# Convolution and SiLU MLP: the up projection by a seven-product block scheme in 64-row tiles

## The chip, the cores and the metric

The kernel runs on one core of one Trainium2 chip. What is measured is the device time of one execution in microseconds (us). Beside the timed runs there is one profiled execution, in which the hardware records every instruction of every engine; all rows shown come from it. Engines are named as in the profile: PE is TensorE (its weight loads, PEld, are a row of their own), DVE is VectorE, ACT is ScalarE, POOL is GpSimd, and SP is the engine whose queue issues most transfers here.

## The reference

Two steps. The first is a causal convolution over the sequence, with seven taps for each of 8 heads (24 channels a head), the taps being a softmax of the weights. The second is an MLP: up from 192 to 2048 channels, SiLU, and down to 192. Everything is fp32.

```python
x: (8, 4096, 192)   weight: (8, 7)   w_in: (192, 2048)   w_out: (2048, 192)
w = softmax(weight, axis=-1)                  # 7 taps per head
conv[b, s, h, :] = sum_k w[h, k] * x[b, s + k - 6, h, :]   # zeros before the start
h = conv.reshape(32768, 192) @ w_in           # "up"
g = h / (1 + exp(-h))                         # SiLU
out = g @ w_out                               # "down"
```

The two weight matrices arrive in 8-byte floats and are rounded to fp32 on the chip, by integer arithmetic on VectorE (`round_w`).

## The kernel before

The 32768 tokens are worked off in 64 blocks of 512. A block goes through these stages:

- `load` (L78): x comes in by eight transfers on SP's queue, in pieces of 32 tokens by 32 channels. `turn_in` (L187) transposes 32x32 squares on VectorE, so that channels lie on the 128 rows (partitions) and tokens along the row. 192 channels make one piece of 128 rows and one of 64; the 64 are held twice, in the lower and the upper half of the rows. Six boundary tokens of the block before are put in front (L184, on POOL).
- `conv` (L198, L200): seven taps for each of the two pieces, one multiplication and six multiply-adds of 128x512 on VectorE.
- Up: the 2048 channels are 16 chunks of 128. For a chunk, `up_a` (L207) contracts the 128-row piece and `up_b` (L215) adds the remaining 64 rows into the same PSUM bank. `up_b` runs for two chunks at a time, one on the lower 64 rows of the array and one on the upper 64: a product on 64 rows uses half of the array, and two on different halves can run side by side.
- `act` (L225): ScalarE reads the bank and writes SiLU of it to SBUF as `g`, one instruction of 128x512 a chunk.
- Down: `down` (L234) contracts each chunk's `g` with w_out, four pieces of 128 tokens, each 192 columns, into two accumulator banks that are open for the whole block.
- `store`: VectorE copies the accumulators (L246), one transfer writes the block.

A block handles its chunks in two groups of eight: four L207, eight L215 (four that finish the first four chunks, four that begin the next four), four L207, then the down products of the eight. PSUM has eight banks: six rotate for h, two are the accumulators.

The program text is unrolled. A planner, ahead of the run, gives every engine a fixed order of instructions and puts the waits between engines; the order of the text counts as priority, but where it reckons an instruction ready early it puts it earlier. So the transposes of a coming block stand directly behind the taps of the one before, and in the first block the rounding steps, transposes and taps are interleaved. At run time each engine takes its queue in that order. A tile can be written again only when a buffer of its pool (`bufs`) is free: all readers of the earlier content are done.

In the first block the weights are loaded and rounded: eight passes (`round_w`, L129 to L149) of twelve VectorE instructions of 768 columns each. One pass covers the up and down weights of two chunks.

Of the kernel before, what the change touches and what calls it, by code (L numbers as in the profile page):

```python
# [16 lines left out]
def kernel(  # L17
# [20 lines left out]

    nc = tc.nc
# [7 lines left out]
    R = D - P  # L47
    grp = D // H
    pad = K - 1
    SUBS = 4  # L50
    TB = P * SUBS
    NB = NT // TB
    NCH = DFF // P
    NQ = NCH // 2
    GA = 4
    assert NCH % (2 * GA) == 0 and GA % 2 == 0
    assert R == 64 and D == H * grp and S % TB == 0 and DFF == 2 * P * NQ and NQ >= 3

    SQ = 32
# [4 lines left out]
    wpool = ctx.enter_context(tc.tile_pool(name="wp", bufs=3))  # L64
    xpool = ctx.enter_context(tc.tile_pool(name="xp", bufs=3))
    gpool = ctx.enter_context(tc.tile_pool(name="gp", bufs=3 * GA))
    opool = ctx.enter_context(tc.tile_pool(name="op", bufs=2))
    ps_h = ctx.enter_context(tc.tile_pool(name="ps_h", bufs=6, space=PSUM))
    ps_o = ctx.enter_context(tc.tile_pool(name="ps_o", bufs=1, space=PSUM))

    nats, xts, cvs, hs, gs, accs = ({} for _ in range(6))

    def load(b):
        nat = nats[b] = xpool.tile([P, 2, TB // SQ, SQ], F32, tag="nat", name="nat")
        for half in range(2):
            for i in range(P // SQ):
                c = SQ * i if half == 0 else P + SQ * i % R
                nc.sync.dma_start(  # L78
                    out=nat[SQ * i : SQ * i + SQ, half, :, :], in_=x_v[b][:, :, c : c + SQ]
                )  # L80

    load(0)


    wraw = const.tile([P, 2, K], F32, name="wraw")
    for half, p0, c0, c1 in ((0, 0, 0, P), (1, 0, P, D), (1, R, P, D)):
        c = c0
        while c < c1:
            h = c // grp
            e = min((h + 1) * grp, c1)  # L90
            p = p0 + c - c0
            nc.scalar.dma_start(
                out=wraw[p : p + e - c, half, :],
                in_=weight[h : h + 1, :].to_broadcast([e - c, K]),
            )
            c = e
# [3 lines left out]
    WA, WB, WO = 2 * P, 3 * P, 3 * P + 2 * D  # L100
    in32 = moe_w_in.bitcast(I32)
    out32 = moe_w_out.bitcast(I32).rearrange("(q e p) d -> q p e d", e=2, p=P)
    raws = {}

    def load_w(q):
        raw = raws[q] = wpool.tile([P, 2 * WO], I32, tag="raw", name="raw")
        nc.gpsimd.dma_start(out=raw[:, 0 : 2 * WA], in_=in32[0:P, 4 * P * q : 4 * P * q + 4 * P])  # L107
        for e in range(2):
            c = 2 * P * (2 * q + e)
            nc.gpsimd.dma_start(  # L110
                out=raw[R * e : R * e + R, 2 * WA : 2 * WB], in_=in32[P:D, c : c + 2 * P]
            )
        nc.gpsimd.dma_start(  # L113
            out=raw[:, 2 * WB : 2 * WO].rearrange("p (e d) -> p e d", e=2), in_=out32[q]
        )

    ws = [const.tile([P, WO], F32, name=f"w{q}") for q in range(NQ)]

    def round_w(q):
        words = raws.pop(q).rearrange("p (n t) -> p n t", t=2)  # L120
        lo, hi = words[:, :, 0], words[:, :, 1]
        sc, ex, mh, ml, st = (
            wpool.tile([P, WO], I32, tag=f"w_{n}", name=f"w_{n}", bufs=1)
            for n in ("sc", "ex", "mh", "ml", "st")
        )
        m = wpool.tile([P, WO], F32, tag="w_m", name="w_m", bufs=1)

# [24 lines left out]

    def w_in_a(q, e):
        return ws[q][:, ts(e, P)]

    def w_in_b(q, e):
        return ws[q][R * e : R * e + R, WA:WB]

# [150 lines left out]
```

## Time and profile before

| | |
|---|---|
| median of 3 runs | 2759.59 us (2758.9 to 2760.28) |
| the profiled execution's own time | 2759.42 us |
| its span, first to last instruction | 2757.4 us |
| TensorE (PE) busy | 2708.0 us, 98% |
| weight loads (PEld) busy | 1908.8 us, 69% |
| VectorE (DVE) busy | 765.9 us, 28% |
| ScalarE (ACT) busy | 573.2 us, 21% |
| GpSimd (POOL) busy | 36.0 us, 1% |
| granted TensorE clock, mean | 0.998 of full |

How to read the rows. In a row of the page's group list stand the line of the kernel, the engine, the operation, what it writes and reads (by the program's names), the shapes, the count; then busy time in us and the mean of one in ns; then the idle time of the engine before these instructions, and what ended most of it. In a timeline row stand the start in us, the length in us, engine, line, operation and count; neighbours of one kind are merged, and a bracket names the idle time before and what released it. A windows row gives a stretch of time, its length, the busy time (and count) of PE, PEld, DVE, ACT and POOL, the granted clock, the share of the DMA engines that was busy, and GB/s. A row of transfers gives the count, the size of one and the median time from issue to landing. Matmuls are pipelined: the length of one is more than its distance to the next, so distances between starts are the better price.

### The profile page before, as it was taken

How to read it: one execution, taken by the hardware profiler on the slowest of the kernel's cores; microseconds unless marked ns; L12 is line 12 of the kernel's file. 1: busy time of each engine (PE TensorE's matmuls, PEld its weight loads, DVE VectorE, ACT ScalarE, POOL GpSimd, SP SyncE). 2: the span in 40 equal slices, each digit the busy share in tenths (PEclk: the TensorE clock that was granted, in tenths of full speed). 3: DMA queues.
4: the chain of work that ended last, by engine and by line, in shares of the span. 5: the costliest groups of instructions: out<-in, count | busy, mean ns of one | idle time of the engine just before them, and what ended most of it. 6: DMA issues, size and time to landing. Idle time of an engine off the chain costs nothing.

```text
span 2757.4 us, 29182 instructions
## 1 busy us (share of the span) xinstructions
PE 2708.0 (98%) x12288; PEld 1908.8 (69%) x12288; DVE 765.9 (28%) x1254; ACT 573.2 (21%) x1027; POOL 36.0 (1%) x100
## 2 busy tenths in 40 slices
PE   3999999999999999999999999999999999999999
PEld 2666776776677667767776776677667767776776
DVE  8613223223133132231231321322313313223120
ACT  1122112211221221122112211221221122112211
POOL 3000000000000000000000000000000000000000
PEclk9999999999999999999999999999999999999999
DMA  5211011011110110110101101101101011000000
GB/s 130 37 27 27 14 27 27 14 27 22 19 27 14 27 28 14 28 27 14 27 19 22 27 14 27 27 14 27 26 15 28 15 26 27 14 19 12 6 12 12
DMA packets 306711, 66.92 MB, mean 24 GB/s; under 512 B 272276, under 2 KB 305172, under 8 KB 306580
## 3 DMA queue, kind: packets, MB, share of 16 engines
q1 hardware_dynamic: 304128, 58.76, 10.8%
q0 software_dynamic: 2048, 6.29, 0.8%
q8 instruction: 96, 1.57, 0.2%
q14 instruction: 35, 0.29, 0.0%
q10 hardware_dynamic: 404, 0.01, 0.0%
HBM read 39.85 MB, written 25.17 MB: 24 GB/s over the span
## 4 chain that ended last, share of the span: by engine, by line
PE 97%; DVE 3%; DMA 0%; issue 0%; DVEq 0%
PE acc L234 48%; PE h L207 32%; PE h L215 17%; DVE cv L200 1%; DMA nat<-in_x_dram 0%; DVE w_ex L129 0%; DVE w L149 0%; DVE w_m L146 0%; DVE w_m L143 0%; DVE w_sc L136 0%; DVE w_st L142 0%; DVE w_st L141 0%; DVE w_sc L129 0%; DVE w_mh L129 0%; DVE w_ml L140 0%
## 5 line engine op out<-in xcount | busy, mean ns | idle before, releaser
L234 PEld LDWEIGHTS acc<-w,g 128*128 128x128 f32 x8192 | 1338.1, 190 | 67.2 <-issue 62.7
L234 PE MATMUL acc<-w,g 128*128 128x192 f32 x8192 | 1353.7, 326 | 1.4 <-ACT g L225 1.4
L225 ACT ACTIVATE g<-h 128x512 f32<-128x512 f32 x1024 | 570.4, 600 | 2158.0 <-PE h L215 1837.3
L207 PE MATMUL h<-cv,w 128*128 128x512 f32 x2048 | 938.3, 601 | 40.3 <-DVE w L149 40.3
L207 PEld LDWEIGHTS h<-cv,w 128*128 128x128 f32 x2048 | 375.6, 190 | 506.0 <-issue 465.1
L198 DVE TENSOR_SCALAR cv<-xt,taps 128x512 f32<-128x512 f32 x128 | 56.6, 483 | 1889.2 <-PE h L207 1889.2
L200 DVE SCALAR_TENSOR_TENSOR cv<-xt,taps,cv 128x512 f32<-128x512 f32 x768 | 514.8, 745 | 0.0
L215 PE MATMUL h<-cv,w 64*128 64x512 f32 x2048 | 476.0, 603 | 3.4 <-DVE w L149 3.4
L215 PEld LDWEIGHTS h<-cv,w 64*128 64x128 f32 x2048 | 198.6, 186 | 270.6 <-issue 247.0
L246 DVE COPY osb<-acc 128x384 f32<-128x384 f32 x128 | 63.7, 532 | 85.0 <-PE acc L234 84.6
L187 DVE STREAM_TRANSPOSE xt<-nat 128x512 f32<-128x512 f32 x128 | 83.8, 691 | 5.0
L184 POOL COPY xt<-xt 128x12 f32<-128x12 f32 x56 | 12.5, 223 | 2171.6 <-DVE cv L200 2146.3
L110 POOL DMA_DIRECT2D raw<-in_moe_w_in_dram x16 | 9.5, 603 | 0.0
L129 DVE TENSOR_SCALAR w_ex<-w_ex 128x768 int32<-128x768 int32 x16 | 8.8, 549 | 0.0
L136 DVE TENSOR_TENSOR w_sc<-w_sc,w_ex 128x768 int32<-128x768 int32 x8 | 7.6, 946 | 0.0
L149 DVE SCALAR_TENSOR_TENSOR w<-w_m,w_sc 128x768 f32<-128x768 f32 x8 | 7.5, 943 | 0.0
L146 DVE SCALAR_TENSOR_TENSOR w_m<-w_mh,w_m 128x768 f32<-128x768 int32 x8 | 7.5, 940 | 0.0
L143 DVE SCALAR_TENSOR_TENSOR w_m<-w_ml,w_st 128x768 f32<-128x768 int32 x8 | 7.5, 937 | 0.0
L107 POOL DMA_DIRECT2D raw<-in_moe_w_in_dram x8 | 6.4, 803 | 38.7 <-DVE w_st L141 37.9
L129 DVE TENSOR_SCALAR w_ex<-raw 128x768 int32<-128x768 int32 x8 | 4.4, 551 | 7.8 <-DMA raw<-in_moe_w_out_dram 7.8
L113 POOL DMA_DIRECT2D raw<-in_moe_w_out_dram x8 | 6.3, 791 | 0.3 <-DMA raw<-in_moe_w_out_dram 0.3
L182 POOL MEMSET xt<- 128x12 f32 x8 | 1.2, 145 | 293.9 <-DVE cv L200 293.9
(18 smaller groups left out, 26.2 us busy)
## 6 DMA issues: line engine op xcount, KB each, us to landing
nat<-in_x_dram SPq DMA_DIRECT2D x512, 64.0 KB, 2.4
out_dram<-osb SPq DMA_DIRECT2D x64, 384.0 KB, 2.8
raw<-in_moe_w_out_dram POOLq DMA_DIRECT2D x8, 384.0 KB, 5.1
raw<-in_moe_w_in_dram POOLq DMA_DIRECT2D x8, 256.0 KB, 3.8
raw<-in_moe_w_in_dram POOLq DMA_DIRECT2D x16, 64.0 KB, 3.2
wraw<-in_weight_dram ACTq DMA_DIRECT2D x9, 0.7 KB
wraw<-in_weight_dram ACTq DMA_DIRECT2D x2, 0.4 KB
wraw<-in_weight_dram ACTq DMA_DIRECT2D x1, 0.2 KB
```

The costliest lines, as they stand in the source:

```text
L110: nc.gpsimd.dma_start(out=raw[R * e : R * e + R, 2 * WA : 2 * WB], in_=in32[P:D, c : c + 2 * P])
L129: nc.vector.tensor_scalar(out, in_, scalar1=s1, scalar2=s2, op0=op0, op1=op1)
L136: nc.vector.tensor_tensor(sc, sc, ex, op=ALU.bitwise_or)
L184: nc.gpsimd.tensor_copy(xt[:, :, 0:pad], xts[b - 1][:, :, TB : TB + pad])
L187: nc.vector.transpose(xt[:, half, pad : pad + TB], nat[:, half, :, :].rearrange("p k c -> p (k c)"))
L198: nc.vector.tensor_scalar(dst, src[:, 0:TB], scalar1=tap, scalar2=None, op0=ALU.mult)
L200: nc.vector.scalar_tensor_tensor(out=dst, in0=src[:, k : k + TB], scalar=tap, in1=dst, op0=ALU.mult, op1=ALU.add)
L207: nc.tensor.matmul(hs[b, c], w_in_a(c // 2, c % 2), cvs[b][:, 0, :], start=first, stop=not first)
L215: nc.tensor.matmul(hs[b, 2 * q + e], w_in_b(q, e), cvs[b][R * e : R * e + R, 1, :], start=first, stop=not first,)
L225: nc.scalar.activation(gs[b, c], hs.pop((b, c)), AF.Silu)
L234: nc.tensor.matmul(accs[b][s // 2][:, s % 2, :], g[:, ts(s, P)], w_out(c), start=c == 0 and s % 2 == 0, stop=c == NCH - 1, skip_group_chec ...
L246: nc.vector.tensor_copy(osb[:, 2 * i : 2 * i + 2, :], acc)
```

## The change

Blocks become 1024 tokens (two halves of 512, called n = 0 and 1). The 192 channels become three thirds of 64 rows. x is held as 128 rows, of which the lower 64 are one third of the channels for the first token half and the upper 64 the same third for the second half; so the convolution works on three pieces of 128x512 for 1024 tokens. Its results are then copied by transfers on SP (`dups`), so that each third of each token half lies on the lower and on the upper 64 rows.

The 16 chunks of 128 output channels become 8 pairs: chunk m with chunk 8 + m. For a pair, the two token halves and the first two thirds of the contraction, the up products form a 2x2 by 2x2 block product; from the second block on (`up_pair`) it is computed with seven products instead of eight (P1 to P7). It needs combinations of the weights (`combine`, once, on POOL), of the convolved input (`win`, four subtractions on VectorE a block), and of the results: U2, U3 and the final sums, five additions of 128x512 on VectorE for each pair, one operand in PSUM, and one copy on ScalarE. The last third is done plainly, four products (E11, E12, E21, E22). Every product is on 64 rows; the order written out in `up_pair` puts one on each row half in every slot. The first block does the plain twelve products (`up_plain`).

All PSUM tiles come from one pool of eight banks. Down is the same products in another order of chunks, eight pieces of 128 tokens in four accumulator banks. Rounding takes eight VectorE and two ScalarE instructions a pass; w_in and w_out are rounded separately. x, convolution and output tiles have one buffer each.

```diff
-    TB = P * SUBS
-    NB = NT // TB
+    TB = 512
+    TT = 2 * TB
+    SUBS = TT // P
+    NB = NT // TT
...
+    xpool = ctx.enter_context(tc.tile_pool(name="xp", bufs=1))
+    gpool = ctx.enter_context(tc.tile_pool(name="gp", bufs=NCH))
+    upool = ctx.enter_context(tc.tile_pool(name="up", bufs=6))
+    psum = ctx.enter_context(tc.tile_pool(name="ps", bufs=8, space=PSUM))
...
+    def rounded(dst, key):
...
+        nc.vector.tensor_single_scalar(ex, hi, 0x7FF * one, op=ALU.bitwise_and)
+        nc.vector.tensor_single_scalar(st, lo, 0xFF, op=ALU.bitwise_and)
+        nc.vector.tensor_scalar(
+            ex, ex, scalar1=float(896 * one), scalar2=float(1151 * one), op0=ALU.max, op1=ALU.min
+        )
+        nc.scalar.sign(st, st)
+        nc.scalar.activation(ex, ex, AF.Copy, bias=-float(896 * 8 * one), scale=8.0)
...
+    def combine(j):
+        def comb(out, u, v, op):
+            nc.gpsimd.tensor_tensor(out, u, v, op=op)
+        s, r = ws[j], wr[j]
+        comb(s[:, 1, 0, :], s[:, 1, 0, :], s[:, 1, 1, :], ALU.add)
+        comb(s[:, 0, 0, :], s[:, 1, 0, :], s[:, 0, 0, :], ALU.subtract)
...
     def turn_in(b):
...
+        for k in range(NK):
             nc.vector.transpose(
+                xt[:, k, pad : pad + TB], nat[:, k, :, :].rearrange("p k c -> p (k c)")
             )
+        nc.sync.dma_start(out=xt[R:P, :, 0:pad], in_=xt[0:R, :, TB : TB + pad])
+        if (b + 1) * TT % S:
+            tails[b + 1] = xpool.tile([R, NK, pad], F32, tag="tail", name="tail", bufs=2)
+            nc.sync.dma_start(out=tails[b + 1], in_=xt[R:P, :, TB : TB + pad])
...
+    def conv(b, k):
...
+        for n in range(2):
+            for e in range(2):
+                nc.sync.dma_start(
+                    out=dups[b][R * e : R * e + R, n, k, :], in_=cvs[b][R * n : R * n + R, k, :]
+                )
...
+    def win(b):
+        d = dups[b]
+        t = wins[b] = xpool.tile([P, 4, TB], F32, tag="win", name="win")
+        for i, u, v in (
+            (0, d[:, 1, 0, :], d[:, 0, 0, :]),
+            (1, d[:, 1, 1, :], t[:, 0, :]),
+            (2, d[:, 1, 1, :], d[:, 1, 0, :]),
+            (3, d[:, 0, 1, :], t[:, 1, :]),
+        ):
+            nc.vector.tensor_tensor(t[:, i, :], u, v, op=ALU.subtract)
...
+    def up_pair(b, j):
+        d, t = dups[b], wins[b]
+        r, s = wr[j], ws[j]
+        prods = {
+            "P1": (0, r[:, 0, 0, :], d[:, 0, 0, :], "b", True),
+            "P2": (0, r[:, 0, 1, :], d[:, 0, 1, :], "b", False),
+            "E11": (0, r[:, 0, 2, :], d[:, 0, 2, :], "b", False),
+            "P7": (0, r[:, 1, 0, :], t[:, 2, :], "c", True),
+            "P4": (0, r[:, 1, 1, :], t[:, 3, :], "c", False),
+            "E21": (0, r[:, 1, 2, :], d[:, 0, 2, :], "c", False),
+            "P6": (1, s[:, 0, 0, :], t[:, 1, :], "a", True),
+            "P5": (1, s[:, 1, 0, :], t[:, 0, :], "d", True),
+            "E22": (1, s[:, 1, 2, :], d[:, 1, 2, :], "d", False),
+            "P3": (1, s[:, 0, 1, :], d[:, 1, 1, :], "d", False),
+            "E12": (1, s[:, 0, 2, :], d[:, 1, 2, :], "d", False),
+        }
...
+        def after(e, name):
+            top, low = 2 * j + e, NM + 2 * j + e
+            if name == "P1":
+                us[e, 2] = upool.tile([P, TB], F32, tag="u", name="u")
+                nc.scalar.copy(us[e, 2], bk[e, "b"])
+            elif name == "E11":
+                nc.scalar.activation(g_tile(b, top)[:, 0, :], bk[e, "b"], AF.Silu)
+            elif name == "U2":
+                add(us[e, 2], us[e, 2], bk[e, "a"])
+            elif name == "U3":
+                us[e, 3] = upool.tile([P, TB], F32, tag="u", name="u")
+                add(us[e, 3], us[e, 2], bk[e, "c"])
+            else:
+                c, n, u, bn = {
+                    "E22": (low, 1, 3, "d"), "E21": (low, 0, 2, "c"), "E12": (top, 1, 2, "d")
+                }[name]
+                g = g_tile(b, c)[:, n, :]
+                add(g, us[e, u], bk[e, bn])
+                nc.scalar.activation(g, g, AF.Silu)
+        for slot, then in (
+            (((0, "P1"), (0, "P6")), ((0, "P1"),)),
+            (((0, "P7"), (0, "P5")), ((0, "U2"), (0, "U3"))),
+            (((1, "P6"), (1, "P1")), ((1, "P1"),)),
+            (((1, "P5"), (0, "E22")), ((0, "E22"), (1, "U2"))),
+            (((1, "E22"), (1, "P7")), ((1, "U3"), (1, "E22"))),
+            (((0, "P2"), (1, "P2")), ()),
+            (((0, "E11"), (0, "P3")), ((0, "E11"),)),
+            (((0, "P4"), (0, "E12")), ((0, "E12"),)),
+            (((0, "E21"), (1, "E11")), ((0, "E21"), (1, "E11"))),
+            (((1, "P3"), (1, "P4")), ()),
+            (((1, "E12"), (1, "E21")), ((1, "E12"), (1, "E21"))),
+        ):
+            for e, name in slot:
+                mm(e, name)
+            for e, name in then:
+                after(e, name)
...
     for b in range(NB):
+        for j in range(NJ):
             if b == 0:
+                round_in(j)
...
+                up_plain(b, j)
+            else:
+                up_pair(b, j)
+        if b == 0:
+            for q in range(NCH // 4):
+                round_out(q)
...
+        if b + 1 < NB:
+            turn_in(b + 1)
+            if b + 2 < NB:
                 load(b + 2)
+            for k in range(NK):
+                conv(b + 1, k)
+            win(b + 1)
+        if b == 0:
+            for j in range(NJ):
+                combine(j)
+        accs = down(b)
+        store(b, accs)
```

341 lines of the change are left out of this document (183 added, 158 removed).

## The prediction

> **What bounds the kernel now.** I read the page's totals first, then the chain that ended last, then the costliest groups.
>
> ```profile
> span 2757.4 us, 29182 instructions
> PE 2708.0 (98%) x12288; PEld 1908.8 (69%) x12288; DVE 765.9 (28%) x1254; ACT 573.2 (21%) x1027; POOL 36.0 (1%) x100
> PE 97%; DVE 3%; DMA 0%; issue 0%; DVEq 0%
> L234 PE MATMUL acc<-w,g 128*128 128x192 f32 x8192 | 1353.7, 326 | 1.4 <-ACT g L225 1.4
> L225 ACT ACTIVATE g<-h 128x512 f32<-128x512 f32 x1024 | 570.4, 600 | 2158.0 <-PE h L215 1837.3
> L207 PE MATMUL h<-cv,w 128*128 128x512 f32 x2048 | 938.3, 601 | 40.3 <-DVE w L149 40.3
> L200 DVE SCALAR_TENSOR_TENSOR cv<-xt,taps,cv 128x512 f32<-128x512 f32 x768 | 514.8, 745 | 0.0
> L215 PE MATMUL h<-cv,w 64*128 64x512 f32 x2048 | 476.0, 603 | 3.4 <-DVE w L149 3.4
> L246 DVE COPY osb<-acc 128x384 f32<-128x384 f32 x128 | 63.7, 532 | 85.0 <-PE acc L234 84.6
> L187 DVE STREAM_TRANSPOSE xt<-nat 128x512 f32<-128x512 f32 x128 | 83.8, 691 | 5.0
> L136 DVE TENSOR_TENSOR w_sc<-w_sc,w_ex 128x768 int32<-128x768 int32 x8 | 7.6, 946 | 0.0
> ```
>
> TensorE is busy for 98% of the span and holds 97% of the chain; VectorE and ScalarE are idle for over 70%. Each fp32 matmul call is two instructions (1024 calls of L207 are 2048). So only TensorE time counts, as long as nothing new makes it wait. The timeline of TensorE in the middle of the run gives its rhythm (start, length up to the last result, line, count):
>
> ```profile
> 1012.38 10.56 PE L234 MATMUL acc<-w,g 128*128 128x192 f32 x64
> 1022.78 3.60 PE L207 MATMUL h<-cv,w 128*128 128x512 f32 x8
> 1026.31 3.70 PE L215 MATMUL h<-cv,w 64*128 64x512 f32 x16
> 1029.94 3.70 PE L207 MATMUL h<-cv,w 128*128 128x512 f32 x8
> 1033.48 10.56 PE L234 MATMUL acc<-w,g 128*128 128x192 f32 x64
> ```
>
> One round, 1012.38 to 1033.48, is 21.10 us: 10.40 of down and 10.70 of up (3.53 + 3.63 + 3.54). It covers 512 tokens and half of the 2048 channels, so 1024 tokens cost 84.4 us: 41.6 down, 42.8 up. The two ends of the run (last down, last copy):
>
> ```profile
> 27.74 3.40 PE L207 MATMUL h<-cv,w 128*128 128x512 f32 x4 [27.74 <-DVE w L149]
> 94.45 3.60 PE L207 MATMUL h<-cv,w 128*128 128x512 f32 x8
> 2742.44 10.56 PE L234 MATMUL acc<-w,g 128*128 128x192 f32 x64
> 2752.39 1.21 DVE L246 COPY osb<-acc 128x384 f32<-128x384 f32 x2 [40.99 <-PE acc L234]
> 0.00:50.00 50.00, 18.81 (x72) 11.23 (x72) 41.55 (x74) 6.15 (x9) 20.83 (x35) 1.00 0.67 148
> 50.00:100.00 50.00, 36.15 (x138) 21.11 (x140) 48.67 (x81) 6.56 (x12) 4.23 (x6) 0.90 0.25 53
> 1000.00:1084.60 84.60, 84.60 (x387) 59.86 (x386) 22.09 (x36) 17.82 (x32) 0.39 (x2) 1.00 0.11 22
> ```
>
> The first 512 tokens last until 94.45; the other 63 blocks take 126 rounds, 2658.6 us, and end at 2753.0; copy and store add 4.4. In the first 100 us VectorE (fourth number of a windows row, 41.55 and 48.67 of 50) rounds the weights and TensorE (the second) waits. In the steady stretch TensorE is busy for all of 84.60 us, VectorE for 22.09.
>
> **The change, part by part.** *Up.* A pair of chunks, two token halves and three thirds of the contraction would be 12 products of 64 rows. The new scheme replaces the 8 products of the first two thirds by 7 and keeps 4 of the last: 11, so 1/12 of the up work goes, not 1/8. A block has 8 chunk pairs, 88 products, issued as 44 slots of two, one on each row half. Their price has a row now, the weight loads inside an L215 run, where two 64-row tiles go side by side:
>
> ```profile
> 2693.61 0.19 PEld L215 LDWEIGHTS h<-cv,w 64*128 64x128 f32 x2 [0.24 <-issue]
> 2694.04 0.19 PEld L215 LDWEIGHTS h<-cv,w 64*128 64x128 f32 x2 [0.23 <-issue]
> 2694.47 0.19 PEld L215 LDWEIGHTS h<-cv,w 64*128 64x128 f32 x2 [0.23 <-issue]
> 2694.89 0.19 PEld L215 LDWEIGHTS h<-cv,w 64*128 64x128 f32 x2 [0.24 <-issue]
> 2694.29 2.06 ACT L225 ACTIVATE g<-h 128x512 f32<-128x512 f32 x4 [14.29 <-PE h L215]
> ```
>
> Three steps take 1.28 us, 0.427 for one instruction on each half, so a slot (two instructions on each) is 0.853. 44 slots are 37.6 us. The run of 16 lasts 3.63 against 8 x 0.427 = 3.41, so entering 64-row tiles costs about 0.2, once a block now; L207's 3.53 puts about 0.1 on the change between up and down. Up is 37.9, down stays 41.6 (the same 256 instructions), a block 79.5 instead of 84.4: 4.9 us, for 31 blocks 152 us.
>
> The skill speaks against pricing by perfect pairs. The Trainium skill (TensorE: Matmul & The Clock Gate, "Measured speedup vs the span model") gives 3.07x, not 4x, for four row tiles of 512 columns. At that efficiency, an estimate from the page, 37.6 would become 49.0, the block 90.9 and the time 2938; rival C is that case. In the trace the pair of halves steps at the 0.427 of the four rows above, so I take the row.
>
> *New VectorE work.* Each chunk pair adds five additions of 128x512, one operand in PSUM; a channel group j (two pairs, 11 slots, 9.4 us) has ten. No such instruction is in the trace. Bounds: the PSUM copy of 384 columns, 532 ns, below; the 768-column two-operand L136, 946 ns, above. I take 745 ns, the 512-column two-operand L200: 7.5 us of 9.4. At 946 ns they would fill 9.5 us, the break-even, so even the upper bound stalls little. The slots leave room: the sum from the fourth slot is needed out of its bank before the seventh, 1.7 us for two additions; the last two banks of a group are wanted three slots, 2.6 us, after their last product, and need two additions, 1.5.
>
> ScalarE gets a copy per pair and keeps four 512-column Silu: ten instructions of 600 ns, 6.0 of 9.4 us. A wait there holds the Silu queued behind it, and then a bank; cover is 3.4 us a group.
>
> *Convolution and its copies.* Per 1024 tokens, three pieces of seven taps instead of four, three transposes instead of four, four subtractions: VectorE 21 + 4 two-operand-like and 3 transposes. Steady rows of now:
>
> ```profile
> 1012.65 0.88 DVE L198 TENSOR_SCALAR cv<-xt,taps 128x512 f32<-128x512 f32 x2 [31.19 <-PE h L207]
> 1013.45 8.03 DVE L200 SCALAR_TENSOR_TENSOR cv<-xt,taps,cv 128x512 f32<-128x512 f32 x12
> 1021.58 1.30 DVE L187 STREAM_TRANSPOSE xt<-nat 128x512 f32<-128x512 f32 x2
> 1066.39 4.04 SPq L78 DMA_DIRECT2D nat<-in_x_dram  x7
> nat<-in_x_dram SPq DMA_DIRECT2D x512, 64.0 KB, 2.4
> out_dram<-osb SPq DMA_DIRECT2D x64, 384.0 KB, 2.8
> L184 POOL COPY xt<-xt 128x12 f32<-128x12 f32 x56 | 12.5, 223 | 2171.6 <-DVE cv L200 2146.3
> ```
>
> Twelve taps in 8.03 are 0.66 apiece back to back: conv 3 x (0.4 + 6 x 0.66) = 13.1, transposes 1.9, subtractions 2.6: 17.6 us, beside 41.6 of down. The next block's row copies (12 transfers of 128 KB on SP) cannot overwrite their one buffer before the last up product, so they start with down: at 0.58 us an issue (4.04 for 7) and 2.8 to land, 10 us. If the conv of the block after waits for them, 10 + 17.6 is still under 41.6: hidden, cover 14 us. SP's x loads, 12 for 1024 tokens instead of 16, stand behind them and are wanted a block later. PSUM is now one pool of eight banks: the four accumulators are free again, by copies of 0.53, by the third slot of the next block, 1.7 us in. Cost zero; without the cover it is 0.5 us a block.
>
> *First block.* It runs the plain 12 products. A rounding pass is four one-operand and four two-operand steps, with two steps on ScalarE, instead of eight and four. Rows of three consecutive steps:
>
> ```profile
> 59.88 0.55 DVE L129 TENSOR_SCALAR w_mh<-raw 128x768 int32<-128x768 int32 x1
> 60.35 0.95 DVE L136 TENSOR_TENSOR w_sc<-w_sc,w_ex 128x768 int32<-128x768 int32 x1
> 61.22 0.55 DVE L140 TENSOR_SCALAR w_ml<-raw 128x768 int32<-128x768 int32 x1
> ```
>
> 0.47 and 0.87 from start to start: 5.4 us a pass instead of 7.2, eight passes 43 instead of 58. Before the first product stand one pass, the transposes, the small copy of the six boundary tokens (2.4 by the nat row), one conv piece of 4.4 and its row copy (2.8): I take a first product at 26, as 27.74 now; the other two conv pieces hold TensorE for about 2 more, a cold clock for 2 (its four first instructions took 3.40). 48 slots are 41.0, down 41.6: 113 us. Passes of 6 us, with the ScalarE steps in them, keep ahead of groups of 10.2 us. Bounds: 105 with no wait, 140 if every pass after the first stood 4 us in TensorE's way. Now 1024 tokens end at 94.45 + 42.2 = 136.7. The twenty weight combinations on POOL, unpriced in the trace (its only copy, L184, has 12 columns), have the first down to hide in: they cost nothing up to 2 us each.
>
> **Sum.** 113 + 31 x 79.5 (2464.5) + 4.8 for the last copies and store = 2582.3 of span; the profiled execution took 2759.42 for its span of 2757.4, 2.0 more, so 2584. It stands 0.2 us under the median of 2759.59.
>
> **Rivals.**
>
> *A. The additions come late in some slots.* Chain: product, ScalarE copy, two or three additions, the next product into the same bank. For it: five ordered steps where there was one Silu, and VectorE at 80% in this stage; one filler instruction of 0.66 ahead of an addition eats a third of the 1.7 us. Against: 14.29 us of ScalarE idle now and slack at every place I priced. At 0.66 us a group, one late addition, 2.6 us a block, 82 us: 2666.
>
> *B. VectorE becomes the bound of the up stage: slower.* The order of the VectorE queue is planned ahead; if it puts the next conv between the additions, up holds 29.8 + 17.6 = 47.4 us of VectorE work against 37.9 of TensorE. The block becomes 89.0 and the time 113 + 2759 + 7 = 2879. It decides from 43.5 us of VectorE work in up, where the 5.6 us a block gained in all (175 / 31) are used up. For it: now the taps are issued as soon as a buffer is free. Against: that buffer comes free only with the row copies at the start of down. The Trainium skill (TensorEngine Tiling (Array Packing), "PSUM Bottleneck") warns of just this, that packing speeds the array but not the emptying of PSUM.
>
> *C. The halves fall apart: slower.* If a product waits alone while its partner runs, the slot costs 1.71 instead of 0.853. With a quarter of the slots so, 11 x 0.853 = 9.4 us a block, 2875; break-even at 6.6 of 44. Against: L215's runs stay paired now, though their products also wait for banks; but they have no VectorE step between them.
>
> *D. The count is right but the start is not:* the first block at 140 instead of 113, 2611. It lies inside the forecast's own range.
>
> **Numbers.** Forecast with D 0.69, A 0.17, B 0.08, C 0.06. Less than 0.2%, 5.5 us, cannot be told from no change. Faster: the forecast and A but for its worst end, 0.85; same 0.02; slower: B and C nearly whole, 0.13. The predicted time is 2584. The forecast's own range is 2566 (first block 105, block 79.2) to 2640 (first block 140, 80.4 a block); A's middle extends the 8-in-10 range to 2685, leaving most of B and C and the worst of A out.
>
> **What would show it.** Right: TensorE over 97% busy, up stretches of 176 instructions in about 38 us between down stretches of 41.6, additions of 0.7 to 0.75 us, taps and subtractions inside down, a first pair product of the second block near 113. A shows as idle TensorE in front of up products, released by VectorE; B as taps between additions and VectorE busy through up; C as up stretches with TensorE busy but far over 38 us. Wrong altogether: a block over 84.4 us.

## The result and the profile after

The changed kernel takes 2642.19 us (median of 4 runs, 2641.86 to 2644.18) against 2759.44 us of the kernel before, measured beside it (2758.9 to 2760.28). The ratio is 0.9576, 95% interval 0.956 to 0.9593: 117 us less. The forecast was 2584, 175 us less; its own range was 2566 to 2640, widened to 2685 for rival A.

The page of the changed kernel, its totals, the chain and the groups of the new additions:

```profile
span 2640.4 us, 34007 instructions
PE 2576.4 (98%) x13840; PEld 2045.2 (77%) x13840; DVE 1466.8 (56%) x2270; ACT 780.4 (30%) x1355; POOL 33.7 (1%) x77
PE 97%; DMA 1%; DVE 1%; POOL 0%; ACT 0%; issue 0%; ACTq 0%; SPq 0%; DVEq 0%; POOLq 0%
L334 DVE TENSOR_TENSOR g<-u,ps 128x512 f32<-128x512 f32 x744 | 491.4, 684 | 231.6 <-PE ps L328 227.2
L334 DVE TENSOR_TENSOR u<-u,ps 128x512 f32<-128x512 f32 x496 | 331.9, 685 | 185.3 <-ACT u L340 170.5
```

TensorE still sets the time. VectorE's busy time has nearly doubled, from 765.9 to 1466.8 us; most of what is new are the 1240 additions of L334, at 684 ns where the forecast took 745. TensorE's timeline shows where the span goes, first at the beginning, then in the middle:

```profile
43.46 6.57 PE L292 MATMUL ps<-dup,wr 64*128 64x512 f32 x16 [43.46 <-DMA dup<-cv]
53.38 10.20 PE L292 MATMUL ps<-dup,wr 64*128 64x512 f32 x32 [3.35 <-DMA dup<-cv]
76.66 34.46 PE L292 MATMUL ps<-dup,wr 64*128 64x512 f32 x144 [13.08 <-ACT g L302]
111.05 41.87 PE L384 MATMUL ps<-wo,g 128*128 128x192 f32 x256
152.85 0.69 PE L328 MATMUL ps<-dup,wr 64*128 64x512 f32 x1
...
1034.28 0.69 PE L328 MATMUL ps<-dup,wr 64*128 64x512 f32 x1
...
1049.21 0.69 PE L328 MATMUL ps<-dup,ws 64*128 64x512 f32 x1
1049.41 0.59 PE L328 MATMUL ps<-dup,wr 64*128 64x512 f32 x1
1049.75 0.59 PE L328 MATMUL ps<-dup,ws 64*128 64x512 f32 x1
...
1072.58 41.87 PE L384 MATMUL ps<-wo,g 128*128 128x192 f32 x256
1114.38 0.69 PE L328 MATMUL ps<-dup,wr 64*128 64x512 f32 x1
```

A block in the middle runs from 1034.28 to 1114.38: 80.10 us, 38.30 of up and 41.80 of down. The second block begins at 152.85 instead of 113. With 31 blocks of 80.10, what is left of the span is 4.45, nearly all of it the last copies and the store. So the 58 us that the forecast has too little are 39.85 in the first block and 31 x 0.6 = 18.6 in the others, less 0.35 at the end.

**The first block.** Three things are late. First, the first product, at 43.46 instead of 26. VectorE's and SP's rows:

```profile
14.07 0.56 DVE L132 TENSOR_SCALAR w_ex<-raw 128x768 int32<-128x768 int32 x1 [7.68 <-DMA raw<-in_moe_w_in_dram]
21.09 0.55 DVE L132 TENSOR_SCALAR w_ex<-raw 128x768 int32<-128x768 int32 x1
28.92 0.70 DVE L233 STREAM_TRANSPOSE xt<-nat 128x512 f32<-128x512 f32 x1
32.92 8.82 DVE L251 SCALAR_TENSOR_TENSOR cv<-xt,taps,cv 128x512 f32<-128x512 f32 x12
31.35 8.67 SPq L83 DMA_DIRECT2D nat<-in_x_dram  x12
41.10 15.02 SPq L256 DMA_DIRECT2D dup<-cv  x12
```

Rounding starts only at 14.07, when the weights have landed. Then a whole second pass (21.09 to 27.5) and the beginning of a third stand ahead of the third transpose, and the taps of two convolution pieces are interleaved, so that neither is done before 41. On SP's queue twelve loads of x for the second block are issued ahead of the first row copy; they end at 40.0, in time for these late pieces and in the way of earlier ones.

Second, TensorE stands for 13.08 us, released at 76.66 by a Silu. ScalarE's rows around it, and the step on VectorE that precedes:

```profile
70.32 0.56 DVE L133 TENSOR_SCALAR w_st<-raw 128x768 int32<-128x768 int32 x1 [1.31 <-DMA raw<-in_moe_w_out_dram]
73.86 0.84 ACT L138 ACTIVATE w_ex<-w_ex 128x768 int32<-128x768 int32 x1 [2.10 <-DVE w_ex L134]
74.72 1.28 ACT L302 ACT_TABLE_LOAD   x1
76.01 2.07 ACT L302 ACTIVATE g<-ps 128x512 f32<-128x512 f32 x4
```

The banks were full at 63.6 and their Silu could have begun then. But in ScalarE's queue the two steps of seven rounding passes stand ahead of the first Silu, and the seventh, of w_out, has its first VectorE step at 70.32. A queue runs in its order, so the Silu begins at 76.01.

Third, the clock. Windows of the same execution (stretch; busy time of PE, PEld, DVE, ACT, POOL; granted clock; DMA):

```profile
63.60:76.60 13.00, 0.00 (x0) 0.00 (x0) 11.69 (x17) 5.24 (x7) 3.14 (x5) 0.58 0.79 175
76.60:90.00 13.40, 13.34 (x48) 11.21 (x50) 13.40 (x22) 8.26 (x16) 0.00 (x0) 0.77 0.01 2
```

Over the wait the granted clock averages 0.58, and over the stretch behind it 0.77. From 43.46 to 111.05 are 67.59 us; less the two waits 51.16 remain for 192 instructions, which take 41.40 in the warm twelve-product run below. The 9.8 us over it are three slow starts, some 3.3 us each. Behind the two waits the granted clock shows it (0.73 from 53.38 to 63.60, and 0.77 above). For the first start it does not: the windows give 1.00 from 43.46 to 50.03, though 16 instructions take 6.57 us there, where the warm pace of 41.40 for 192 gives 3.5. That this start too is slow by the clock is argued from the like pace, not shown.

**The other blocks.** The product at 1049.21 is P3 of the first pair in its group. It writes into the bank that the addition for E22 reads:

```profile
1046.48 2.08 DVE L334 TENSOR_TENSOR u<-u,ps 128x512 f32<-128x512 f32 x3 [1.17 <-ACT u L340]
1048.48 0.68 DVE L334 TENSOR_TENSOR g<-u,ps 128x512 f32<-128x512 f32 x1
```

This addition ends at 1049.16, and P3 follows. Three additions stand ahead of it on VectorE, not two: behind U2 and U3 of the first pair the third can only be U2 of the second pair, which the planner put in front of the E22 sum. Without its 0.60 us the sum would have ended at 1048.56, before P3's turn at 1049.41 - 0.43 = 1048.98, when its partner started (an estimate from these rows; that order was not run). The other half did not wait: its next instruction starts at 1049.41, the partner only at 1049.75, and the two halves stay 0.34 us apart. It happens once a block and is most of the 0.4 us by which up is longer than 37.9.

### The profile page after: what moved, and what is told of

Its sections match the earlier page's. It is cut to its first block, busy times and chain, and to the rows that moved or that the text cites. A ratio compares the mean times of both kernels' runs of the same rounds, so it can differ in the third digit from the quotient of the medians.

```text
span 2640.4 us, 34007 instructions
## 1 busy us (share of the span) xinstructions
PE 2576.4 (98%) x13840; PEld 2045.2 (77%) x13840; DVE 1466.8 (56%) x2270; ACT 780.4 (30%) x1355; POOL 33.7 (1%) x77
## 4 chain that ended last, share of the span: by engine, by line
PE 97%; DMA 1%; DVE 1%; POOL 0%; ACT 0%; issue 0%; ACTq 0%; SPq 0%; DVEq 0%; POOLq 0%
PE ps L384 51%; PE ps L328 45%; PE ps L292 1%; DVE cv L251 1%; DMA raw<-in_moe_w_in_dram 0%; DMA nat<-in_x_dram 0%; DMA ws<-wr 0%; DMA raw<-in_moe_w_out_dram 0%; POOL ws L173 0%; DMA xt<-xt 0%; DVE w_ex L151 0%; POOL raw L115 0%; DVE w_mh L148 0%; DVE xt L233 0%; DVE w_ex L132 0%
## 5 line engine op out<-in xcount | busy, mean ns | idle before, releaser
L384 PEld LDWEIGHTS ps<-wo,g 128*128 128x128 f32 x8192 | 1330.3, 190 | 24.3 <-issue 24.3
L384 PE MATMUL ps<-wo,g 128*128 128x192 f32 x8192 | 1339.8, 326 | 0.0
L328 PE MATMUL ps<-dup,wr 64*128 64x512 f32 x1984 | 736.9, 591 | 0.0
L328 PE MATMUL ps<-dup,ws 64*128 64x512 f32 x1488 | 679.8, 591 | 0.0
L334 DVE TENSOR_TENSOR g<-u,ps 128x512 f32<-128x512 f32 x744 | 491.4, 684 | 231.6 <-PE ps L328 227.2
L354 ACT ACTIVATE g<-g 128x512 f32<-128x512 f32 x744 | 461.6, 630 | 415.1 <-DVE g L334 414.7
L328 PE MATMUL ps<-win,wr 64*128 64x512 f32 x992 | 505.0, 589 | 0.0
L328 PEld LDWEIGHTS ps<-dup,wr 64*128 64x128 f32 x1984 | 308.9, 187 | 201.0 <-issue 138.0
L334 DVE TENSOR_TENSOR u<-u,ps 128x512 f32<-128x512 f32 x496 | 331.9, 685 | 185.3 <-ACT u L340 170.5
L328 PE MATMUL ps<-win,ws 64*128 64x512 f32 x992 | 427.1, 592 | 0.0
L292 PE MATMUL ps<-dup,wr 64*128 64x512 f32 x192 | 51.2, 683 | 59.9 <-DMA dup<-cv 46.8
L292 PEld LDWEIGHTS ps<-dup,wr 64*128 64x128 f32 x192 | 39.2, 219 | 71.1 <-DVE w_mh L148 43.4
```

The costliest lines, as they stand in the source:

```text
L292: nc.tensor.matmul(hs[a, n, e], rows(wr[j], e)[:, a, k, :], rows(d, e)[:, n, k, :], start=k == 0, stop=k == NK - 1,)
L328: nc.tensor.matmul(bk[e, bn], rows(w, half), rows(v, half), start=first, stop=True, skip_group_check=True,)
L334: nc.vector.tensor_tensor(out, u, v, op=ALU.add)
L354: nc.scalar.activation(g, g, AF.Silu)
L384: nc.tensor.matmul(accs[s // 2][:, s % 2, :], g[:, ts(s, P)], wo[c // 4][:, c % 4, :], start=i == 0 and s % 2 == 0, stop=i == NCH - 1, ski ...
```

## The experiments

In the expectations, Theory 1 is this reading: the scheme runs at its price in the steady blocks but for the slip of P3, and the rest was lost in the first block to the order of queues. The rivals are named with each.

| kernel | time, us | ratio to the kernel before, 95% interval |
|---|---|---|
| changed kernel | 2642.19 | 0.9576 (0.956 to 0.9593) |
| twelve products | 2738.13 | 0.9922 (0.9907 to 0.9937) |
| twelve products, halves in turn | 3667.59 | one run |
| every addition twice | 3199.33 | 1.1594 (1.157 to 1.1617) |
| four more additions, early | 2847.45 | 1.0319 (1.0302 to 1.0337) |
| four more additions, late | 2638.93 | 0.9562 (0.9548 to 0.9577) |
| P3 a slot later | 2633.76 | 0.9542 (0.9528 to 0.9557) |
| rounding without ScalarE | 2629.11 | 0.9526 (0.9512 to 0.954) |
| start in order | 2629.32 | 0.9526 (0.951 to 0.9542) |
| these three together | 2617.00 | 0.9484 (0.9469 to 0.9498) |
| and two further queues mended | 2600.91 | 0.9426 (0.9413 to 0.9439) |

### Is it the seven products? Twelve in their place

```diff
             else:
-                up_pair(b, j)
+                up_plain(b, j)
...
-            win(b + 1)
-        if b == 0:
-            for j in range(NJ):
-                combine(j)
```

In `up_plain` every group after the first of all takes its products output by output.

> The scheme undone: every block does the plain twelve products of 64 rows, no combinations, no additions, the rest as in the changed kernel. Theory 1 (the shortfall of 58 us lies in the first block, 40 us, and in 0.6 us a block; a product slot is worth 0.853 us and the additions cost nothing but a slip of 0.24 us a block): up becomes 48 slots, 41.0 + 0.2, a block 83.2 instead of 80.1, the time 152.9 + 31 x 83.2 + 6.2 = 2738 us. Theory 2 (the additions on VectorE slow the products by more than the slip, some 2 us a block hidden in the length of up): the block gains only 1 to 2 us without the scheme less, 81 to 82, 2670 to 2700 us.

Measured 2738.13 us (2737.49 to 2739.74). The second block of this kernel:

```profile
152.43 41.47 PE L292 MATMUL ps<-dup,wr 64*128 64x512 f32 x192
193.83 41.87 PE L384 MATMUL ps<-wo,g 128*128 128x192 f32 x256
```

Up takes 41.40 us for 48 slots, 0.8625 each, and a block 83.2. Going from twelve products to eleven, with all that the scheme adds on VectorE and ScalarE, is worth 2738.13 - 2642.19 = 96 us, 3.1 a block. Of the change's 117 us the other 21 come from what else was changed, the layout above all: 31 blocks at 83.2 instead of 84.4 are 37 us, and the first block gives back 15.7 (152.43 instead of the 136.7 of the kernel before).

### Rival C in full: one row half after the other

```diff
-        for k, (a, n) in order:
-            for e in range(2):
+        todo = [(k, o, (0, 1)) for k, o in order]
+        if b:
+            todo = [(k, o, (e,)) for e in range(2) for k, o in order]
+        for k, (a, n), es in todo:
+            for e in es:
```

This is the twelve-product kernel; from the second block on, each group does all its products on one half and then all on the other.

> The twelve-product kernel of the first experiment, with the order of the matmuls changed from the second block on: all products of one row half, then all of the other, so that consecutive products lie on the same 64 rows. This is the rival in which the halves fall apart, in its full extent. If two halves overlap only when neighbouring instructions lie on different halves, an instruction takes 0.853 us instead of 0.427, the up stretch 96 x 0.853 = 81.9 us instead of 41.4, and the time 2738 + 31 x 40.5 = 3990 us. If the sequencer lets a later product of the other half pass or overlap anyway, it stays near 2738.

Measured 3667.59 us in the one run. Up took 1130.66 - 1059.31 = 71.35 us. The steps inside it show in the weight loads:

```profile
1059.31 71.42 PE L295 MATMUL ps<-dup,wr 64*128 64x512 f32 x192
1130.66 41.87 PE L387 MATMUL ps<-wo,g 128*128 128x192 f32 x256
...
1067.57 0.19 PEld L295 LDWEIGHTS ps<-dup,wr 64*128 64x128 f32 x1 [0.24 <-issue]
1068.00 1.16 PEld L295 LDWEIGHTS ps<-dup,wr 64*128 64x128 f32 x7 [0.24 <-issue]
1069.39 0.19 PEld L295 LDWEIGHTS ps<-dup,wr 64*128 64x128 f32 x1 [0.24 <-issue]
```

On one half alone an instruction steps at 0.43 us, which is what two take when they lie on different halves. So a partner costs nothing, and without it half the array is lost. The expectation of 81.9 us was too high because at each border seven loads go into 1.39 us: some instructions of the next half start while the last of the other still run. The borders save 192 x 0.43 - 71.35 = 11 us a block. The rival's mechanism is real, its price a little lower than forecast; it did not happen in the changed kernel, whose halves stay paired but for the 0.34 us above.

### Rivals A and B: how much VectorE work does up bear?

Three kernels. The first does every addition twice, the first time into a spare tile or into its own target. The second does the addition U3 three times, so that a group has fourteen additions instead of ten; U3 stands ahead of the E22 sum, for whose bank P3 waits. The third has the slots of the next section (P3 later) and also fourteen additions a group, but the new ones stand behind the sum for E21 of each pair:

```diff
-                add(us[e, 3], us[e, 2], bk[e, "c"])
+                for _ in range(3):
+                    add(us[e, 3], us[e, 2], bk[e, "c"])
```
```diff
                 add(g, us[e, u], bk[e, bn])
+                if name == "E21":
+                    for _ in range(2):
+                        junk = upool.tile([P, TB], F32, tag="junk", name="junk", bufs=2)
+                        add(junk, us[e, u], bk[e, bn])
```

> The changed kernel with every addition done twice: 20 a group. Theory B (VectorE becomes the bound of up when its work exceeds the group's 9.44 us, 15.7 additions at 0.60): up is VectorE's 20 x 0.60 = 12.0 us a group or a little more, 48 to 52 us, a block 90 to 94, time 2945 to 3075 us. If the additions ran beside TensorE without bound, the time would stay under 2700 us.

> The changed kernel with the addition U3 done three times in each pair, 14 additions a group of 11 slots instead of 10. Theory A (what an addition costs is the delay of the one product that waits behind it: P3 has no slack and gets two more additions, 1.2 us, ahead of it in each of four groups): 4 to 5 us a block, 84 to 85 us, time 2765 to 2800 us, slower than the kernel before. Theory B (VectorE counts only when its work fills the group: 14 x 0.60 is 8.4 of 9.44 us): less than 0.5 us a block, 2642 to 2655 us.

> The same four extra additions a group (into a tile that nobody reads), but behind E21, the last addition of each pair, and in the order with P3 one slot later. Theory A (position decides: these delay the next group's chain by at most 1.2 us, of which P3's new slack of 0.85 takes most): at most 0.4 us a group over 79.76, 79.8 to 81.2 us a block, time 2634 to 2678 us, far from fill2's. Theory C (amount decides, not position: every extra addition costs its time because VectorE's queue is in step with TensorE): like fill2, 84 us a block or more, 2765 us or more.

Measured 3199.33, 2847.45 and 2638.93 us. The second against the changed kernel costs 205 us, 6.6 a block. The third against its own slots without the additions, 2633.76, costs 5.2, which is 0.17 a block. In both VectorE has four additions more in a group, 2.4 us at 0.60 each, and 2.9 in the second kernel, where each writes the tile of the one before and takes 0.72. The waits of the second kernel (what waits, for what; us in total, times, longest) and the product that begins late in each group:

```profile
PEld ps L328 <- DVE g L334: 247.7, 248, 1.9
PE ps L328 <- DVE g L334: 61.6, 93, 1.0
...
1037.37 0.69 PE L328 MATMUL ps<-dup,ws 64*128 64x512 f32 x1 [0.66 <-DVE g L334]
1048.78 0.69 PE L328 MATMUL ps<-dup,ws 64*128 64x512 f32 x1 [0.66 <-DVE g L334]
```

A group lasts 1048.78 - 1037.37 = 11.41 us instead of 9.4, with VectorE at some 9 us of work. TensorE's own row shows only 61.6 us of waiting, because the other half is still busy; the row of the weight loads, where the product waits, has the 247.7. So the place of an addition decides here, before the engine is full: in the third kernel VectorE is busy for 8.70 of a group's 9.44 us, and that costs next to nothing. Part of its place is that P3 has a slot more there; the four additions were not tried at the third kernel's place with the old slots. The expectation for the second kernel was 2765 to 2800 by rival A; two late banks in each group make it more.

The first kernel is rival B come true. In up VectorE goes from addition to addition (a pair every 1.3 to 1.4 us), and TensorE waits for it:

```profile
PE 2838.7 (89%) x13840; PEld 2016.5 (63%) x13840; DVE 2292.8 (72%) x3510; ACT 778.4 (24%) x1355; POOL 33.2 (1%) x77
PE ps L328 <- DVE g L339: 293.1, 124, 3.1
```

It is above the 2945 to 3075 expected. Twenty additions at 0.66 are 13.2 us a group, not the 12 that 0.60 gives, as a step takes 0.72 where it writes what the last one wrote. Groups last some 14 us; TensorE, busy for 89% only, had a granted clock of 0.937 over the run, and what of the rest is the clock and what the place of the additions was not taken apart.

### The 0.6 us of the steady block: P3 a slot later

```diff
-            (((0, "E11"), (0, "P3")), ((0, "E11"),)),
-            (((0, "P4"), (0, "E12")), ((0, "E12"),)),
-            (((0, "E21"), (1, "E11")), ((0, "E21"), (1, "E11"))),
+            (((0, "E11"), (1, "E11")), ((0, "E11"), (1, "E11"))),
+            (((0, "P4"), (0, "P3")), ()),
+            (((0, "E21"), (0, "E12")), ((0, "E21"), (0, "E12"))),
```

> One change of order: P3 of the first pair, the product that must wait until the addition for E22 has read its bank, is put one slot later (slots 7 to 9 become E11/E11, P4/P3, E21/E12). Theory 1 (P3 stands 0.24 us behind that addition once a block, and the two halves stay apart by 0.34 us until the block's end): up falls from 38.30 to 38.0, a block to 79.8, the time by 31 x 0.3 = 9 us to 2633. Theory 2 (the extra 0.6 us a block are a cost of entering and leaving 64-row tiles, or of the slot itself): no change, 2642 us. Theory 3 (the additions move with the order and another bank comes late): slower by 5 to 30 us.

Measured 2633.76 us (2632.84 to 2634.44), where 2633 was expected. Its span is 2631.9 us and its second block begins at 155.03, so a block is (2631.9 - 4.45 - 155.03) / 31 = 79.76 us: 0.34 less than in the changed kernel, 10.5 us in all. The first block, in which nothing was edited, ends 2.2 us later (155.03 instead of 152.85), so that the gain shows as 8.4; why it does was not tried. Up is 37.96, the 37.9 of the forecast. Down stays at 41.80 for 41.6; what its 0.2 are was not tried.

### The first block, cause by cause

First, rounding's two ScalarE steps go to VectorE, so that no Silu stands behind one:

```diff
-        nc.scalar.sign(st, st)
-        nc.scalar.activation(ex, ex, AF.Copy, bias=-float(896 * 8 * one), scale=8.0)
+        nc.vector.tensor_single_scalar(st, st, 1, op=ALU.min)
+        nc.vector.tensor_scalar(
+            ex, ex, scalar1=float(896 * one), scalar2=8.0, op0=ALU.subtract, op1=ALU.mult
+        )
```

> Rounding alone is changed: its two ScalarE steps go to VectorE, so that ScalarE's queue holds nothing but Silu after the first passes. Theory 1 (TensorE's 13.08 us wait in the first block is Silu standing in ScalarE's queue behind steps of later rounding passes): that wait goes or falls under 4 us, the second block starts at 139 to 145 instead of 152.9, time 2628 to 2634 us. Theory 2 (the wait is the rounding work itself, VectorE's passes being the bound): passes get longer by 0.94 us each, the second block starts at 153 to 160, 2642 to 2650 us.

Measured 2629.11 us (2628.65 to 2629.9). The 13 us wait is gone and the second block begins at 139.50, 13.35 us earlier; the wait for the row copies, 3.35 us before, is 6.64 now:

```profile
58.02 39.75 PE L294 MATMUL ps<-dup,wr 64*128 64x512 f32 x172 [6.64 <-DMA dup<-cv]
139.50 0.69 PE L330 MATMUL ps<-dup,wr 64*128 64x512 f32 x1
```

Second, the order of the start: the second weight load on SP behind x, the x of the second block behind the row copies, and every rounding pass but the first behind the convolution of the first block. The planner is bound by pinning an instruction behind the one written before it on its engine:

```diff
-    load_in(1, nc.gpsimd)
+    load_in(1, nc.sync)
...
-    load(1)
     conv(0, 0)
...
                         conv(0, k)
+                    load(1)
...
+            if key != ("i", 0):
+                tc.keep_in_program_order(ins)
```

> Only the order of the first block is changed: the second weight load goes behind x on SP's queue, x of the second block goes behind the row copies of the first, and every rounding pass after the first is held behind the three conv pieces on VectorE. Theory 1 (the first product comes 17 us later than forecast because a whole rounding pass, half of another, and x of the second block were put ahead of conv and its copies): first product at 32 to 37 instead of 43.5, all three conv pieces there by 43 instead of 53, second block from 125 to 140, time 2615 to 2630 us. Theory 2 (the start is bound by the transfers themselves, x and weights landing at 14 us and later): first product not before 41, time within 5 us of 2642.

Measured 2629.32 us (2628.59 to 2629.67). The first product comes at 34.13, and the 48 instructions of the first group run without a stop. Part of it is lost again to Silu held up in ScalarE's queue, now in four waits of 5.63, 2.83, 2.04 and 1.07 us. Ahead of the last three stand rounding steps. Ahead of the first stands, last of all, the issue of the weights' row copies (L166), which waits for a rounding pass:

```profile
34.13 12.51 PE L300 MATMUL ps<-dup,wr 64*128 64x512 f32 x48 [34.13 <-DMA dup<-cv]
52.27 18.80 PE L300 MATMUL ps<-dup,wr 64*128 64x512 f32 x72 [5.63 <-ACT g L310]
49.17 1.12 ACTq L166 DMA_DIRECT2D ws<-wr  x2
```

Third, both, and P3 later:

> The three edits that each gained by itself, together: P3 one slot later, rounding without ScalarE, the order of the first block. Theory 1 (three separate causes: the slip in each block, Silu behind rounding steps, and conv and its copies behind rounding and x loads): first product near 34, no wait of TensorE for Silu over 2 us in the first block, second block from 117 to 122, a block 79.8, time 2595 to 2602 us. Theory 2 (the two start edits removed the same wait twice, since each of them by itself brought the second block to 139.7): second block from 135 to 140, 2617 to 2622 us.

Measured 2617.00 us (2616.17 to 2617.99): not the 2595 to 2602 of Theory 1. The time is the lower end of what its rival gave, but the second block begins at 128.99, not at 135 to 140, so neither reading fits. The first product is at 34.05, but two waits stand behind it, the second of them new. Rows of TensorE, ScalarE's queue and VectorE:

```profile
53.59 33.67 PE L302 MATMUL ps<-dup,wr 64*128 64x512 f32 x144 [6.91 <-ACT g L312]
138.12 1.22 PE L338 MATMUL ps<-win,ws 64*128 64x512 f32 x1 [7.13 <-DVE osb L411]
...
43.45 8.17 ACTq L168 DMA_DIRECT2D ws<-wr  x4
51.65 1.28 ACT L312 ACT_TABLE_LOAD   x1 [45.63 <-DVE w_ex L135]
...
122.53 8.03 DVE L261 SCALAR_TENSOR_TENSOR cv<-xt,taps,cv 128x512 f32<-128x512 f32 x12
137.54 0.98 DVE L411 COPY osb<-ps 128x384 f32<-128x384 f32 x2
```

The first Silu stands, as in the kernel before this, behind the issue of the weights' row copies on ScalarE's queue (L168 here), which wait for rounding. And down ends at 129, but VectorE's copies of the accumulators, which free the banks, stand behind the taps of the third block, from 121.7 to 135.7. In the steady blocks these taps lie well inside down; behind the late first block they do not.

That leaves two explanations of the miss: a further row of queue faults, or VectorE's sum of work as a floor. The last kernel takes the two out: the row copies are issued from SP, and the taps are queued behind the additions of the block before (the x loads of all later blocks are pinned as well; what that does alone was not tried, and the blocks keep their length).

```diff
-            nc.scalar.dma_start(
+            nc.sync.dma_start(
                 out=ws[j][R * e : R * e + R], in_=wr[j][R - R * e : 2 * R - R * e]
...
-            nc.vector.tensor_tensor(out, u, v, op=ALU.add)
+            last[0] = nc.vector.tensor_tensor(out, u, v, op=ALU.add)
...
-                conv(b + 1, k)
+                if b:
+                    with tc.issue_after(last[0].ins):
+                        conv(b + 1, k)
+                else:
+                    conv(b + 1, k)
```

> The kernel with all three edits, and two more: the row copies of the weights are issued from SP's queue instead of ScalarE's, so that no Silu stands behind them; and from the second block on the taps of a block are queued on VectorE behind the additions of the block before, so that the copies of the accumulators and the first additions of the second block stand ahead of them. Theory 1, that the missing time of the first block was a row of separate queue faults, each of which can be taken out: first product at 34 as before, no Silu wait of several us, the first down stretch begins when the third w_out rounding is done, near 82, and ends near 124, the 7.1 us wait for the accumulators is gone, so the second block begins at 123 to 126 and its products run at full rate; with 31 blocks of 79.8 and a tail of 4.5 the span is 2601 to 2604 and the time 2602 to 2606. Theory 2, that VectorE's sum of work in the first block bounds it whatever the order: the gain of the two edits stays under 5 us and the time is 2612 to 2618. If the taps, now later, hold up the row copies of the following blocks, the blocks grow beyond 79.8 and the time rises past 2620.

Measured 2600.91 us (2600.81 to 2601.01), ratio 0.9426. It is the fastest of all, 41 us under the changed kernel:

```profile
34.14 44.71 PE L302 MATMUL ps<-dup,wr 64*128 64x512 f32 x192 [34.14 <-DMA dup<-cv]
78.78 2.87 PE L394 MATMUL ps<-wo,g 128*128 128x192 f32 x16
82.46 39.27 PE L394 MATMUL ps<-wo,g 128*128 128x192 f32 x240 [0.81 <-DVE wo L160]
121.65 0.69 PE L338 MATMUL ps<-dup,wr 64*128 64x512 f32 x1
```

All 192 instructions of the first block run in one stretch, 3.2 us longer than the warm 41.40; a window from 34.00 to 78.70 gives a clock of 1.00, so here too the first start shows as slow by its pace alone. The second block begins at 121.65, the others take (2599.1 - 4.45 - 121.65) / 31 = 79.77. Of the 41 us, 31.2 are from the first block and 10.2 from the others. VectorE's work as a floor is ruled out; what remains of it is 0.81 us. The two edits were not run apart, but each has its own wait, and both waits are gone. What still keeps the first product at 34 shows in VectorE's rows: a wait for the small copy of the boundary tokens, and the taps of two pieces interleaved.

```profile
22.86 0.88 DVE L255 TENSOR_SCALAR cv<-xt,taps 128x512 f32<-128x512 f32 x2 [3.52 <-DMA xt<-xt]
23.65 8.83 DVE L261 SCALAR_TENSOR_TENSOR cv<-xt,taps,cv 128x512 f32<-128x512 f32 x12
```

## Why the prediction was right or wrong

**Direction and cause: right.** The bound stayed TensorE (98% busy), and the gain is that of fewer 64-row products: 96 of the 117 us by the twelve-product run. Its size was two thirds of the forecast's 175.

**The range: held by luck.** 2642 lies above the forecast's own 2640. It lies under 2685 only because the range was widened for rival A, and A cost 0.34 us a block instead of 2.6. What made the time long was the first block.

**The slot of 0.853 us and up of 37.9: right.** P3 a slot later gives 37.96 us of up. The Trainium skill (TensorE: Matmul & The Clock Gate, "Measured speedup vs the span model") has 3.07x for four row tiles. Carried over to two halves, that gave the forecast's estimate of 2938. These runs do not bear out the carrying over: 0.43 us for an instruction alone, 0.427 for one on each half, a speedup of two for two.

**The additions: safe in length, wrong at one place.** They take 684 ns with 0.60 from start to start, not 745, so VectorE has about 6 of 9.4 us to do in a group. The forecast did price the bank that E22's sum frees for P3 of the first pair, "1.7 us for two additions", but the planner put a third addition ahead of that sum. That is rival A in small, with the filler instruction that A named: 0.34 us once a block where A had 2.6. The step that failed is the steady block of 79.5, by 0.6: 0.34 by the slip of P3, 0.06 in the rest of up, and 0.2 in down.

**The sum of VectorE work as the test for rival B: wrong.** It was to decide from 43.5 us of VectorE work in an up stage. Fourteen additions a group are some 35 us in an up stage, and that kernel is at 2847, slower than before; the same number at another place costs 5 us. A bank that is wanted back decides, not the sum. Doubled additions show that B's mechanism exists. The Trainium skill (TensorEngine Tiling (Array Packing), "PSUM Bottleneck") warns that tiling does not speed up the emptying of PSUM. The doubled kernel agrees with its 293.1 us of waits, while the changed kernel shows none of its size.

**Taps, copies, accumulators and weight combinations: hidden, as forecast**, in the steady blocks: down follows up at once and no wait for them stands in TensorE's rows. Accumulator copies turned into a bound only in the kernel with the three edits, where the start had moved and the taps had not.

**The first block: this is where it failed**, 113 against 152.85. Three terms of its sum (a fourth, "about 2 more" for the other two convolution pieces, came to 3.35):

- "I take a first product at 26": it came at 43.46. The sum added the steps of the first piece as if nothing else stood between them on VectorE and SP. The planner put a second rounding pass, taps of a second piece and the loads of the second block there. With these moved it is 34.1; of the other 8 us some 5 are the second piece whose taps are still interleaved (9.5 us from 22.86 to 32.4 for two, 4.4 for one in the sum) and the rest was not taken apart.
- "Passes of 6 us ... keep ahead of groups of 10.2 us": the passes do, but the Silu waited behind the steps of passes that no product needed yet. The forecast had named such a wait ("A wait there holds the Silu queued behind it, and then a bank") for the steady groups, with cover 3.4, and did not apply it to the first block: 13.08 us.
- "a cold clock for 2": 9.8 us, as TensorE started three times and each start cost some 3.3.

Rival D, which had the first block at 140, was the nearest in kind, and too mild. It and the range took in bounds for the waits of passes, none for the order of two queues.

## What to carry to other kernels

Price the start of a kernel from the order of each queue, not from the sum of the steps: what a product needs may stand behind work that nothing needs yet, and each new start of TensorE came on top, here at some 3.3 us. When a stage gets new vector work, ask for each instruction which bank it frees and when that is wanted; here four additions in the wrong place cost 205 us with the engine not yet full. And when one late start is mended, look at once for what was hidden behind it: the repairs here left two further waits, one of them new.

## What the runs showed of the hardware

- Two 64-row products on different halves cost no more than one: 0.427 us a pair of instructions, 0.43 one alone. At a border between halves the engine lets the next half begin early, some 1.4 us a border (11 us over a block's eight).
- A wait of one half shows only in part as TensorE idle time. In the kernel with early additions TensorE's waits are 61.6 us, those of the weight loads 247.7, and the loss 205.
- Additions of 128x512 with one operand in PSUM start 0.60 us apart when independent and 0.72 when one writes the tile of the last, at a recorded length of 0.68 to 0.69.
- Behind a stop of 13.08 us TensorE had a granted clock of 0.77 over 13.4 us, by estimate 3.1 us lost; the three starts of the changed kernel cost 9.8 us together, and the kernel that starts once has 3.2. For a first start the windows give a clock of 1.00, and only the pace shows it.
